# The last group's v read into k's buffer, the exponential put aside to a later slot, and other places for W4's last read and the sums of W3's blocks

## The chip, the cores and the metric

One core of one Trainium2 chip. The metric is the device time of the whole kernel in microseconds, here the median of three runs. Its engines are named as in the profile: PE (matmul; PEld is its load of weights), DVE (vector), ACT (scalar), POOL (GpSimd) and SP, which here only issues transfers. Each engine takes its own instructions in program order and waits on semaphores for the others.

## The reference

x is 2048 tokens by 576 channels, all in fp32. A layer norm of x feeds two branches, and their results are added to x:

```python
def _A_ref(x, wqkv, wo):                     # attention
    qkv = (x @ wqkv).reshape(B, S, 3, H, Dh) # H = 32 heads of Dh = 18
    idx = pos[:, None] - arange(8) * 2       # 8 keys per query, every second token back
    kg, vg = k[:, :, idx_c, :], v[:, :, idx_c, :]
    logits = einsum("bhsd,bhswd->bhsw", q, kg) * scale   # idx < 0 masked
    attn = softmax(logits)
    o = einsum("bhsw,bhswd->bhsd", attn, vg)
    return o.reshape(B, S, D) @ wo
def _B_ref(x, w1, w2, w3, w4):               # mixer MLP
    h = gelu(layernorm(x) @ w1)
    hs = shifts_of_quarters(h) @ w2          # four quarters of channels, shifted +1 -1 +2 -2 tokens
    x1 = x + hs
    return x1 + gelu(layernorm(x1) @ w3) @ w4   # w3: 576 x 4608, w4: 4608 x 576
xn = layernorm(x)
return x + _A_ref(xn, wqkv, wo) + _B_ref(xn, w1, w2, w3, w4)
```

## The kernel before

Every fp32 product on PE is made of products of two parts: each operand is split into a high part (rounded to the fp32r format, mostly by ACT) and a low part (what is left, mostly by DVE).

**Stages.** QKV: xn times wqkv; q, k and v go to a DRAM buffer qkvd. Then W1, the shifts and W2. Then W3, gelu and W4 for a part of the 4608 hidden channels in a plain loop of 32 units (L960). Then the round loop (L1130): 20 rounds q = 0 to 19, for the rest. Last the output projection by wo. Transfers are issued by SP, but for those that add to DRAM, which POOL issues (L837).

**Attention** runs on DVE beside all of this, from the plain loop on to round 14 at the latest. It is a generator, `attention` (L677), over 8 groups of heads. For a group g: logits by products and sums (L735, L738), the mask, the maximum and its subtraction (L745 to L749), the exponential on ACT (L753, over the tile L), then, a group late, `av(g - 1)` (L699): sum of L (L702), reciprocal (L703), scaling (L705), eight products with v (L711) and seven sums (L715), and the write of the result from tile po to DRAM od by SP (L717; its rows are pieces of 72 floats). q, k and v of a group are read by `load` from qkvd on SP (L692; k and v have a second, leading piece, L695). Each of q, k, v has one buffer, so a read waits until the group ahead is done with the tile: q and k of g + 1 are asked for when the logits of g are issued, v of g when av(g - 1) is.

**bg(us)** (L763) takes the next steps of that generator. It is called after every step of the loops with a budget of microseconds (1.6 in the rounds, less what DVE already got in that step, `spent`), and each step yields its estimated cost. A step that yields None sets `hold`: no later step is issued until a call with `late`, which in the rounds is the one after P6, but not in round 9.

**A round** takes a pair of 128-channel blocks of the hidden layer for one half of the tokens (rounds 0 to 9 the first, 10 to 19 the second, with the pairs in reverse order). P1 to P7 are its seven products of 7 matmuls each (L1065) by a Strassen-like scheme: operands A and S are blocks and combinations of W3 (tiles w3a, w3s), B and T blocks and combinations of the tokens (tiles x1n and xt). Results gather in PSUM banks cc and pass over ACT (`keep`, L1071) and DVE (`z_add`, L1075); gelu is on ACT (L795, L796, L801, L802), the low part on DVE (L807). D0 to D7 are the products of the round before with W4, 12 matmuls each (L832), one for each block of 128 tokens. Their two PSUM banks are emptied in turn, by DVE (L841) for some token blocks and by ACT and POOL (L836, L837) for others; D(n + 2) waits for the emptying of D(n).

The order of a round is written as a string; the ordinary one is `P1 P2 D0 P6 D1 P5 D2 P7 D3 P4 D4 P3 D5 D6 D7`, that of round 9 `P1 P2 P6 P5 P7 D0 P4 P3 D1 ... D7`, that of round 10 `D0 D1 P1 P2 D2 P6 ...`. `at("P7", f)` puts f behind that step on all engines. What is put so:

- `load_w4` (L559): W4 of this pair into two odd halves of the Y tile, on SP; `split_w4`: its high part by ACT (L566) and its low part by DVE (L569), which frees the landing place.
- `load_pair` (L910, L913): the raw block of W3 of a later round into w3st, six issues. `split_a` makes w3a of it (L926, L928 on ACT, L929 on POOL, L932 on DVE), `combine` (L921) four sums in place on DVE, and then `split_s` makes w3s.
- Round 9 reads the seven token operands of the second half (`get_op`, L881, L883: four issues each), and rounds 9 and 10 split them (`split_op`: L892 to L894 on ACT, L594 on DVE), B11 first.
- Rounds 15 to 18 prepare the output projection: `load_o` reads od (L1113), `o_turn` transposes it on DVE (L160, L161), `put_o` writes it to DRAM xd (L168), `read_xo` (L173) reads it back. Round 19 loads wo (L1101, L205).

A transfer on SP also waits until the one issued eight before it has landed, since their completions share eight semaphores.

Of the kernel before, what the change touches and what calls it, by code (L numbers as in the profile page):

```python
# [10 lines left out]
AF = mybir.ActivationFunctionType  # L11
# [46 lines left out]
def fused_block(ctx, tc, x, wqkv, wo, w1, w2, w3, w4, out):  # L58
# [618 lines left out]
    def attention(ap):  # L677
# [19 lines left out]
            return t  # L697

        def av(g):  # L699
            L, v = Ls[g], vs[g]  # L700
            Lf = L.rearrange("p j h w -> p (j h) w")
            dve.tensor_reduce(den[g], Lf, axis=AX.X, op=ALU.add)  # L702
            dve.reciprocal(den[g], den[g])  # L703
            yield 0.8
            dve.tensor_tensor(Lf, Lf, den[g][:, :, None].to_broadcast([128, TPP * GH, W]),  # L705
                              op=ALU.mult)
            yield 0.6
            for w in range(W):
                vv = v[:, DIL * w:DIL * w + TPP, :].rearrange("p j (h d) -> p (j h) d", d=HD)
                dst = prod if w else o  # L710
                dve.tensor_tensor(dst, vv, Lf[:, :, w:w + 1].to_broadcast([128, TPP * GH, HD]),  # L711
                                  op=ALU.mult)
                yield 1.35
                if w:
                    dve.tensor_tensor(o, o, dst, op=ALU.add)  # L715
                    yield 1.35
            sp.dma_start(od.rearrange("(p j) d -> p j d", p=128)[:, :, g * GC:(g + 1) * GC],  # L717
                         po[:, 0, :].rearrange("p (j c) -> p j c", c=GC))
# [5 lines left out]
        for g in range(NG + 1):  # L724
            if g < NG:
                q, k = qs[g], ks[g]
                L = Ls[g] = ap.tile([128, TPP, GH, W], F32, name="L", bufs=2)
                Lf = L.rearrange("p j h w -> p (j h) w")
                Lw = Lf.rearrange("p x w -> p w x")
                qf = q.rearrange("p j d -> p (j d)")  # L730
                for w, n in ((0, 1), (1, 1), (2, 2), (4, 2), (6, 2)):
                    dst = po[:, 2 - n:2, :]
                    win = bass.AP(tensor=k.tensor, offset=k.offset + DIL * w * GC,
                                  ap=[list(k.ap[0]), [DIL * GC, n], [1, TPP * GC]])
                    dve.tensor_tensor(dst, qf[:, None, :].to_broadcast([128, n, TPP * GC]), win,  # L735
                                      op=ALU.mult)
                    yield 0.15 + 1.2 * n
                    dve.tensor_reduce(Lw[:, w:w + n, :],  # L738
                                      dst.rearrange("p w (x d) -> p w x d", d=HD),
                                      axis=AX.X, op=ALU.add)  # L740
                    yield 0.15 + 1.2 * n
                if g + 1 < NG:
                    qs[g + 1], ks[g + 1] = load("q", 0, g + 1, False), load("k", 1, g + 1, True)
                mx = den[g] = ap.tile([128, TPP * GH], F32, name="mx", bufs=2)
                dve.tensor_tensor(L, L, mask4, op=ALU.add)  # L745
                yield 0.6
                dve.tensor_reduce(mx, Lf, axis=AX.X, op=ALU.max)
                yield 0.6
                dve.tensor_tensor(Lf, Lf, mx[:, :, None].to_broadcast([128, TPP * GH, W]),  # L749
                                  op=ALU.subtract)  # L750
                yield 0.6
                yield None
                act.activation(L, L, AF.Exp, scale=float(HD) ** -0.5)  # L753
                if g == 0:
                    yield 4.0
            if g:
                yield from av(g - 1)
                if g < NG:
                    vs[g] = load("v", 2, g, True)

    state = {"gen": None, "debt": 0.0, "hold": False, "done": False}

    def bg(us, late=True):  # L763
        if state["gen"] is None or state["done"]:
            return
        state["debt"] = min(state["debt"] + us, 4.0)
        while state["debt"] > 0 and (late or not state["hold"]):
            cost = next(state["gen"], False)
            if cost is False:
                state["done"] = True  # L770
                return
            state["hold"] = cost is None
            state["debt"] -= cost or 0.0


    def temp(t, n=512):
# [125 lines left out]
    def pair(q):  # L902
        return q if q < NWP else 2 * NWP - 1 - q
# [226 lines left out]
    for q in range(NQ):  # L1130
# [6 lines left out]
        if z == -1:  # L1137
# [3 lines left out]
            wop = tc.tile_pool(name="wop", bufs=1, reuse_waits="tile")  # L1141
            wopool = wop.__enter__()
            Wo = wopool.tile([128, 10, D], F32R, name="Wo")
            load_w4(p)
            for k in range(5):
                load_wo(k)
        if q == NWP:
# [17 lines left out]
        def at(it, f, *args):  # L1165
            plan.setdefault(it, []).append(lambda: f(*args))
# [45 lines left out]
        elif z < -1:  # L1212
            at("P1", load_w4, p)
            at("D1", split_a, n, (0, 1))
            at("D2", split_a, n, (2,))
            at("P7", combine, n)
            at("D3", split_w4, p, 0)
            at("P4", gelu22)
            at("P4", split_w4, p, 1)
# [5 lines left out]
            if z < -2:  # L1225
                at("D6", load_pair, q + 2 + (q == NWP - 2))
        else:
            at("D2", split_w4, p)
            at("D3", gelu22)
            at("D4", low22)  # L1230
            at("D5", gelu12)
            at("D6", low12)
# [9 lines left out]
        if -4 <= z < -1:  # L1242
            at("P1", put_o, z + 4)
        if z == -2:
            at("D7", put_o, 3)

        if z == -1:
# [134 lines left out]
```

## Time and profile before

| | us |
|---|---|
| median of three runs | 1306.22 (1305.91 to 1307.12) |
| the profiled execution, its time | 1301.97 |
| span of its trace | 1300.2 |
| mean granted clock of PE | 0.993 |
| PE busy in the span | 1266.0 |
| DVE busy | 944.6 |
| ACT busy | 598.2 |
| POOL busy | 245.2 |

The span is what the trace covers of one profiled execution; the execution's own time holds a little more at both ends. The three runs without a profile lie some 4 us above it. In rows of the timeline the first number is the start in the span, the second the length from the first instruction's start to the last one's end, then the engine, the line, operation, `out<-in`, shapes, and how many instructions the row groups; in brackets the idle time ahead of it and who ended it. A row of waits says who waited, for whom, then the sum in microseconds, the number of times and the longest. "SPq" is the issue of a transfer on SP. A row of transfers gives KB and the microseconds from issue to landing.

### The profile page before, as it was taken

How to read it: one execution, taken by the hardware profiler on the slowest of the kernel's cores; microseconds unless marked ns; L12 is line 12 of the kernel's file. 1: busy time of each engine (PE TensorE's matmuls, PEld its weight loads, DVE VectorE, ACT ScalarE, POOL GpSimd, SP SyncE). 2: the span in 40 equal slices, each digit the busy share in tenths (PEclk: the TensorE clock that was granted, in tenths of full speed). 3: DMA queues.
4: the chain of work that ended last, by engine and by line, in shares of the span. 5: the costliest groups of instructions: out<-in, count | busy, mean ns of one | idle time of the engine just before them, and what ended most of it. 6: DMA issues, size and time to landing. Idle time of an engine off the chain costs nothing.

```text
span 1300.2 us, 19681 instructions
## 1 busy us (share of the span) xinstructions
PE 1266.0 (97%) x7538; PEld 1161.7 (89%) x7538; DVE 944.6 (73%) x1261; ACT 598.2 (46%) x952; POOL 245.2 (19%) x358
## 2 busy tenths in 40 slices
PE   8999999999999999999999999999959999999999
PEld 8999998899888998989899889999848999988898
DVE  6456535778469999999999889999859654665442
ACT  3322226526534434344346656556546555554530
POOL 2011100021221212222221222222112222222100
PEclk9999999999999999999999999999979999999999
DMA  7646874256887878988788777776796658899972
GB/s 210 156 111 143 172 166 144 71 147 177 203 247 152 174 170 202 233 145 223 146 205 185 136 171 159 154 161 112 161 228 106 129 110 180 174 209 195 255 242 83
DMA packets 201374, 219.16 MB, mean 169 GB/s; under 512 B 79152, under 2 KB 137744, under 8 KB 201152
## 3 DMA queue, kind: packets, MB, share of 16 engines
q1 hardware_dynamic: 168912, 151.57, 41.0%
q0 software_dynamic: 32368, 66.34, 31.9%
q8 instruction: 59, 0.97, 0.3%
q14 instruction: 35, 0.29, 0.1%
HBM read 119.73 MB, written 107.28 MB: 175 GB/s over the span
## 4 chain that ended last, share of the span: by engine, by line
PE 78%; DMA 10%; DVE 4%; issue 4%; ACT 2%; SPq 1%; POOL 0%; DVEq 0%; POOLq 0%; ACTq 0%
PE ps L832 27%; PE ps L214 16%; PE cc L1065 13%; PE p L813 13%; PE ps L466 4%; PE ps L313 3%; DMA w3st<-in_B_w_dram 2%; DMA x1n<-xn 1%; DMA yd<-Y 1%; DMA xn<-st 1%; DMA xt<-xn 1%; DMA w3a<-w3st 1%; DMA xt<-xd 1%; DMA wr<-in_A_wo_dram 1%; PE ps L481 1%
## 5 line engine op out<-in xcount | busy, mean ns | idle before, releaser
L832 PEld LDWEIGHTS ps<-w,c 128*128 128x128 f32 x3456 | 474.5, 188 | 27.5 <-DVE Y L841 8.8
L832 PE MATMUL ps<-w,c 128*128 128x288 f32 x3456 | 486.1, 295 | 10.8 <-DVE Y L841 7.0
L837 POOL DMA_DIRECT2D yd<-Y x154 | 137.0, 894 | 464.7 <-ACT Y L836 388.4
L836 ACT COPY Y<-ps 128x576 f32<-128x576 f32 x154 | 97.9, 636 | 151.4 <-PE ps L832 96.5
L807 DVE TENSOR_TENSOR c<-Y,c 128x512 fp32r<-128x512 f32 x144 | 98.4, 685 | 58.8 <-ACT Y L796 42.3
L214 PE MATMUL ps<-WQ,xt 128*128 128x432 f32 x672 | 134.8, 360 | 0.0
L214 PEld LDWEIGHTS ps<-WQ,xt 128*128 128x128 f32 x672 | 125.6, 188 | 5.7
L1065 PE MATMUL cc<-xt,w3s 128*128 128x512 f32 x420 | 108.3, 398 | 13.5 <-DVE Y L1075 13.5
L841 DVE TENSOR_TENSOR Y<-ps,Y 128x576 f32<-128x576 f32 x108 | 81.2, 751 | 49.2 <-PE ps L832 49.0
L1065 PEld LDWEIGHTS cc<-xt,w3s 128*128 128x128 f32 x420 | 76.7, 190 | 27.6 <-DVE Y L1075 14.0
L711 DVE TENSOR_TENSOR po<-v,L 128x1152 f32<-128x1152 f32 x64 | 86.1, 1353 | 14.7 <-DMA v<-qkvd 13.8
L735 DVE TENSOR_TENSOR po<-q,k 128x2304 f32<-128x2304 f32 (+1 forms) x40 | 82.9, 2073 | 13.9 <-issue 11.6
L795 ACT ACTIVATE c<-p 128x512 fp32r<-128x512 f32 x64 | 38.2, 597 | 115.8 <-PE p L813 115.8
L738 DVE TENSOR_REDUCE L<-po 128x128 f32<-128x2304 f32 (+1 forms) x40 | 82.8, 2069 | 0.4
L1071 ACT COPY Y<-cc 128x512 f32<-128x512 f32 x60 | 35.1, 584 | 97.4 <-PE cc L1065 94.1
L121 POOL TENSOR_TENSOR rs<-rs,mhalf 128x1 f32<-128x1 f32 x48 | 30.9, 643 | 258.8 <-DVE rs L120 148.0
L715 DVE TENSOR_TENSOR po<-po 128x1152 f32<-128x1152 f32 x56 | 75.8, 1353 | 0.8
L323 ACT COPY stg<-ps 128x864 f32<-128x864 f32 x24 | 21.2, 881 | 102.8 <-PE ps L214 60.5
L1065 PE MATMUL cc<-x1n,w3a 128*128 128x512 f32 (+1 forms) x280 | 67.9, 393 | 0.0
L1065 PEld LDWEIGHTS cc<-x1n,w3a 128*128 128x128 f32 (+1 forms) x280 | 51.6, 188 | 10.3
L214 PE MATMUL ps<-W,h 128*128 128x288 f32 x384 | 53.5, 295 | 0.0
L813 PE MATMUL p<-xt,w3s 128*128 128x512 f32 x224 | 52.4, 390 | 0.0
(188 smaller groups left out, 1892.6 us busy)
## 6 DMA issues: line engine op xcount, KB each, us to landing
yd<-Y POOLq DMA_DIRECT2D x156, 288.0 KB, 5.2
Y<-in_B_w_dram SPq DMA_DIRECT2D x27, 576.0 KB, 6.7
w3st<-in_B_w_dram SPq DMA_DIRECT2D x52, 256.0 KB, 6.3
qkvd<-stg SPq DMA_DIRECT2D x24, 432.0 KB, 3.5
yd<-ev POOLq DMA_DIRECT2D x26, 288.0 KB, 6.4
xd<-st SPq DMA_DIRECT2D x16, 320.0 KB, 6.0
xd<-big SPq DMA_DIRECT2D x16, 320.0 KB, 7.4
w3st<-in_B_w_dram SPq DMA_DIRECT2D x76, 64.0 KB, 6.5
```

The lines of the kernel that those rows point to most:

```text
L214: pe.matmul(ps[:, h, :n], xs(a), ws(b, h), start=i == 0, stop=i == len(PAIRS) - 1)
L711: dve.tensor_tensor(dst, vv, Lf[:, :, w:w + 1].to_broadcast([128, TPP * GH, HD]), op=ALU.mult)
L715: dve.tensor_tensor(o, o, dst, op=ALU.add)
L735: dve.tensor_tensor(dst, qf[:, None, :].to_broadcast([128, n, TPP * GC]), win, op=ALU.mult)
L738: dve.tensor_reduce(Lw[:, w:w + n, :], dst.rearrange("p w (x d) -> p w x d", d=HD), axis=AX.X, op=ALU.add)
L807: dve.tensor_tensor(h[:, 1, :], g, h[:, 0, :].bitcast(F32), op=ALU.subtract)
L813: pe.matmul(ps, W3[f][:, w, :], x1n[b][:, a, :], start=n == 0, stop=n == len(PAIRS) - 1)
L832: pe.matmul(ps[:, k, :HF], h[:, col], w[:, p, k * HF:(k + 1) * HF], start=n == 0, stop=n == len(seq) - 1)
L836: act.copy(e.rearrange("p (h c) -> p h c", h=2), ps[:, :, :HF])
L837: pool.dma_start(yd[t], e, accum_op=ALU.add)
L841: dve.tensor_tensor(yv, ps[:, :, :HF], yv, op=ALU.add)
L1065: pe.matmul(ps, WX[w][:k, v, SLOT[w], :], area[sb][xk][:k, a, :], start=onto is None and i == 0, stop=last and i == len(HALVES) - 1, skip_ ...
```

## The change

Four things are done.

1. v of the last group (g = 7) is no longer read into v's buffer behind av(6), but into k's buffer, asked for as soon as the last logits are issued. The other groups are read as before.
2. The exponential is no longer issued where the generator reaches it, and the generator no longer stops there: it is put aside in `state["exp"]` and issued by the next `late` call of bg, or at the next group's exponential, or ahead of av(7).
3. W4 of the last round is read at D7 of round 18, ahead of that round's `put_o`, and no longer at the start of round 19; in round 19 its split and the first gelu come a step later.
4. `combine` goes from P7 to D3 in rounds 1 to 8 and 11 to 18, ahead of the first half of `split_w4`.

```diff
@@ -697,6 +697,8 @@
             return t
 
         def av(g):
+            if g == NG - 1:
+                exp_now()
             L, v = Ls[g], vs[g]
             Lf = L.rearrange("p j h w -> p (j h) w")
             dve.tensor_reduce(den[g], Lf, axis=AX.X, op=ALU.add)
@@ -749,28 +751,36 @@
                 dve.tensor_tensor(Lf, Lf, mx[:, :, None].to_broadcast([128, TPP * GH, W]),
                                   op=ALU.subtract)
                 yield 0.6
-                yield None
-                act.activation(L, L, AF.Exp, scale=float(HD) ** -0.5)
+                exp_now()
+                state["exp"] = lambda L=L: act.activation(L, L, AF.Exp, scale=float(HD) ** -0.5)
+                if g == NG - 1:
+                    vs[g] = load("k", 2, g, True)
                 if g == 0:
                     yield 4.0
             if g:
                 yield from av(g - 1)
-                if g < NG:
+                if g < NG - 1:
                     vs[g] = load("v", 2, g, True)
 
-    state = {"gen": None, "debt": 0.0, "hold": False, "done": False}
+    state = {"gen": None, "debt": 0.0, "exp": None, "done": False}
+
+    def exp_now():
+        if state["exp"]:
+            state["exp"]()
+            state["exp"] = None
 
     def bg(us, late=True):
         if state["gen"] is None or state["done"]:
             return
+        if late:
+            exp_now()
         state["debt"] = min(state["debt"] + us, 4.0)
-        while state["debt"] > 0 and (late or not state["hold"]):
+        while state["debt"] > 0:
             cost = next(state["gen"], False)
             if cost is False:
                 state["done"] = True
                 return
-            state["hold"] = cost is None
-            state["debt"] -= cost or 0.0
+            state["debt"] -= cost
 
 
     def temp(t, n=512):
@@ -1141,7 +1151,6 @@
             wop = tc.tile_pool(name="wop", bufs=1, reuse_waits="tile")
             wopool = wop.__enter__()
             Wo = wopool.tile([128, 10, D], F32R, name="Wo")
-            load_w4(p)
             for k in range(5):
                 load_wo(k)
         if q == NWP:
@@ -1213,7 +1222,7 @@
             at("P1", load_w4, p)
             at("D1", split_a, n, (0, 1))
             at("D2", split_a, n, (2,))
-            at("P7", combine, n)
+            at("D3", combine, n)
             at("D3", split_w4, p, 0)
             at("P4", gelu22)
             at("P4", split_w4, p, 1)
@@ -1225,8 +1234,8 @@
             if z < -2:
                 at("D6", load_pair, q + 2 + (q == NWP - 2))
         else:
-            at("D2", split_w4, p)
-            at("D3", gelu22)
+            at("D3", split_w4, p)
+            at("P4", gelu22)
             at("D4", low22)
             at("D5", gelu12)
             at("D6", low12)
@@ -1242,6 +1251,7 @@
         if -4 <= z < -1:
             at("P1", put_o, z + 4)
         if z == -2:
+            at("D7", load_w4, NPL + pair(q + 1))
             at("D7", put_o, 3)
 
         if z == -1:
```

The orders of PE and POOL stay the same. In the rows below names have the kernel's own counters, and the lines of the changed kernel are 2 to 10 higher: L719 is L717 of before, L891 L881, L920 L910, L931 L921.

SP, rounds 8 and 9, before: from the W3 block's last issues and W4 of round 9 through the first two operands to the third.

```order
L559 DMA Y<-in_B_w_dram 128x2x576
L881 DMA x1n_6401<-xn_98 128x2x512
L883 DMA x1n_6401<-xn_98 32x512 x3
L881 DMA x1n_6401<-xn_98 128x2x512
L883 DMA x1n_6401<-xn_98 32x512 x3
L717 DMA od<-po 2048x1x72
L692 DMA v<-qkvd 128x1152
L695 DMA v<-qkvd 128x1008
L881 DMA xt<-td1T_105 128x2x512
```

The same place now, beginning with W4 of round 7.

```order
L559 DMA Y<-in_B_w_dram 128x2x576
L692 DMA k<-qkvd 128x1152
L695 DMA k<-qkvd 128x1008
L920 DMA w3st<-in_B_w_dram 128x2x256 x2
L923 DMA w3st<-in_B_w_dram 32x2x256 x4
L559 DMA Y<-in_B_w_dram 128x2x576
L920 DMA w3st<-in_B_w_dram 128x2x256 x2
L923 DMA w3st<-in_B_w_dram 32x2x256 x4
L719 DMA od<-po 2048x1x72
L559 DMA Y<-in_B_w_dram 128x2x576
L891 DMA x1n_6402<-xn_98 128x2x512
L893 DMA x1n_6402<-xn_98 32x512 x3
```

The last read of v, two pieces, stood between the second and the third operand of round 9. It stands behind W4 of round 7 now, into k; and od's write of group 6 has come from behind the second operand to a place ahead of W4 of round 9.

DVE, round 18, from the low part of a gelu to the evacuation of a D step, before:

```order
L807 TENSOR_TENSOR c_10357<-Y,c_10357 128x512
L921 TENSOR_TENSOR w3st<-w3st 128x3x128 x4
L160 STREAM_TRANSPOSE big_9924<-Y 128x16x32
L161 STREAM_TRANSPOSE big_9924<-Y 128x4x32
L569 TENSOR_TENSOR w_10285<-Y,w_10285 128x2x576
L841 TENSOR_TENSOR Y<-ps_10423,Y 128x576
```

and now:

```order
L817 TENSOR_TENSOR c_10357<-Y,c_10357 128x512
L160 STREAM_TRANSPOSE big_9924<-Y 128x16x32
L161 STREAM_TRANSPOSE big_9924<-Y 128x4x32
L931 TENSOR_TENSOR w3st<-w3st 128x3x128 x4
L569 TENSOR_TENSOR w_10285<-Y,w_10285 128x2x576
L851 TENSOR_TENSOR Y<-ps_10423,Y 128x576
```

The two transposes stood behind the four sums of W3's block and stand ahead of them now; the low part of W4 still follows.

SP, end of round 18 and beginning of round 19, before:

```order
L559 DMA Y<-in_B_w_dram 128x2x576
L168 DMA xd<-big_9923 32x20x128 x4
L1113 DMA Y<-od 32x576 x4
L168 DMA xd<-big_9924 32x20x128 x4
L559 DMA Y<-in_B_w_dram 128x2x576
L1101 DMA wr<-in_A_wo_dram 128x576 x4
```

and now:

```order
L559 DMA Y<-in_B_w_dram 128x2x576
L168 DMA xd<-big_9923 32x20x128 x4
L1123 DMA Y<-od 32x576 x4
L559 DMA Y<-in_B_w_dram 128x2x576
L168 DMA xd<-big_9924 32x20x128 x4
L1111 DMA wr<-in_A_wo_dram 128x576 x4
```

W4's read and the four writes of `put_o` have changed places.

## The prediction

> **What bounds the kernel now.** I read the page's totals and its chain of waits first, then the waits by engine, then the timeline of each engine around the longest wait, and last the windows and the transfers there.
>
> ```profile
> PE 1266.0 (97%) x7538; PEld 1161.7 (89%) x7538; DVE 944.6 (73%) x1261; ACT 598.2 (46%) x952; POOL 245.2 (19%) x358
> PE 78%; DMA 10%; DVE 4%; issue 4%; ACT 2%; SPq 1%; POOL 0%; DVEq 0%; POOLq 0%; ACTq 0%
> ```
>
> PE works 97% of the span, and this change leaves the matmuls alone: it can win only PE's gaps, which are 1300.2 − 1266.0 = 34.2 us, or make new ones. The waits tell whose they are: of PE first, and then the one row of DVE's that matters.
>
> ```profile
> PE cc L1065 <- DVE Y L1075: 13.5, 1, 13.5
> PE ps L832 <- DVE Y L841: 7.0, 7, 1.5
> PE cc L1065 <- ACT Y L1071: 2.7, 1, 2.7
> ...
> DVE po L711 <- DMA v<-qkvd: 13.8, 1, 13.8
> ```
>
> One gap of 13.5 us is over a third of it all. Seven short ones wait for DVE's evacuation L841. One of 2.7 us waits for ACT. The long one lies in round 9, where the halves of the tokens change. PE there:
>
> ```profile
> 938.93 1.77 PE L1065 MATMUL cc<-x1n,w3s 128*128 128x512 f32 x7
> 940.54 1.75 PE L832 MATMUL ps<-w,c 128*128 128x288 f32 x12
> 942.13 1.79 PE L1065 MATMUL cc<-xt,w3a 128*128 128x512 f32 x7
> 957.45 3.29 PE L1065 MATMUL cc<-xt,w3s 128*128 128x512 f32 x7 [13.54 <-DVE Y L1075]
> 960.57 9.95 PE L832 MATMUL ps<-w,c 128*128 128x288 f32 x72
> 970.88 3.57 PE L832 MATMUL ps<-w,c 128*128 128x288 f32 x24 [0.36 <-ACT Y L836]
> 975.39 1.86 PE L832 MATMUL ps<-w,c 128*128 128x288 f32 x12 [0.94 <-ACT Y L836]
> ```
>
> DVE in the same stretch, then SP, which issues the transfers:
>
> ```profile
> 939.67 0.69 DVE L705 TENSOR_TENSOR L<-L,mx 128x512 f32<-128x512 f32 x1
> 954.17 2.63 DVE L711 TENSOR_TENSOR po<-v,L 128x1152 f32<-128x1152 f32 x2 [13.80 <-DMA v<-qkvd]
> 956.71 0.68 DVE L1075 TENSOR_TENSOR Y<-cc,Y 128x512 f32<-128x512 f32 x1
> ```
>
> ```profile
> 935.77 0.45 SPq L559 DMA_DIRECT2D Y<-in_B_w_dram  x1
> ...
> 945.87 0.53 SPq L717 DMA_DIRECT2D od<-po  x1
> 946.45 2.22 SPq L692 DMA_DIRECT2D v<-qkvd  x1
> ```
>
> The causal chain is plain. v of the last group has one buffer, free only when av of group 6 has ended, as it had before L705 of group 7 at 939.67. Its read stands on SP behind W4 and eight issues of operand reads, goes out at 946.45 and lands at 954.17. DVE has stood in L711 since 940.3, with L1075 behind it, the sum that frees a bank of cc for the next product: PE waits for that until 957.45. ACT:
>
> ```profile
> 945.83 1.06 ACT L892 ACTIVATE x1n<-x1n 128x1024 fp32r<-128x1024 f32 x1 [4.51 <-DMA x1n<-xn]
> ...
> 947.59 0.63 ACT L894 ACTIVATE x1n<-x1n 64x512 fp32r<-64x512 f32 x1
> 962.37 0.64 ACT L836 COPY Y<-ps 128x576 f32<-128x576 f32 x1 [14.15 <-PE ps L832]
> ...
> 967.96 1.04 ACT L892 ACTIVATE xt<-xt 128x1024 fp32r<-128x1024 f32 x1
> ```
>
> The windows (busy time of PE, PEld, DVE, ACT, POOL, then granted clock, share of the DMA engines, GB/s), and the two transfers of one size that landed in 930 to 975:
>
> ```profile
> 943.00:957.00 14.00, 0.92 (x4) 0.38 (x3) 2.83 (x3) 2.31 (x3) 0.00 (x0) 0.64 1.04 285
> ...
> 965.00:970.00 5.00, 5.00 (x38) 4.80 (x37) 4.94 (x6) 4.92 (x8) 0.87 (x1) 1.00 0.75 112
> ```
>
> ```profile
> Y<-in_B_w_dram SPq DMA_DIRECT2D x1, 576.0 KB, 7.2
> ...
> od<-po SPq DMA_DIRECT2D x1, 576.0 KB, 5.5
> ```
>
> While PE stands still the DMA engines are full: whatever ends the wait for v will meet the operand reads. And from 962.37 on ACT is the one that is full (4.92 of 5.00): PE's next two gaps, 0.36 and 0.94, wait for it.
>
> **A: v into k's buffer, and the exponential that stops nothing.** k of group 7 is last read by the logits, so the read of v goes out in round 7, two rounds ahead of its use, far longer than the 7.7 us that it took here (946.45 to 954.17); L711 finds it there. The 13.54 us do not all go, since another chain stands close behind: operand B11 lands at 945.83, ACT's three activations on it end at 947.59 + 0.63 = 948.22, 2.4 us later, and only then, in ACT's order, comes the evacuation L836 that frees a psum bank. Before, L836 began at 962.37 and from it ACT ran without a break to the evacuation that released PE at 975.39: 975.39 − 962.37 = 13.0 us. If that stretch keeps its length and follows B11's three activations at once, the new time of its end is B11's landing + 2.4 + 13.0.
>
> When B11 lands: in the new order od's write stands ahead of W4 and B11 on SP. At least its issue, 0.5 us, is added: 946.3, the end at 961.7, a gain of 13.7. At most it holds the operand up by its whole 5.5 us as well: 951.8, the end at 967.2, a gain of 8.2. Between: the two v reads, 576 + 504 KB, leave this stretch, but they were issued behind B11, so they do not help it; od's 0.59 MB at 285 GB/s take 2.1 us. With 0.5 + 2.1 B11 lands at 948.4, the end is 963.8. I take **−11.5** (13.7 … 8.2). The later operands are close: T2's read goes out when the eighth issue before it has landed, as od's did before (945.87, behind B11's 945.83), so near 948.4, lands some 7 us later (W4's row), near 955.5, and ACT wants it at 967.96 − 11.6 = 956.4.
>
> [...]
>
> **B: W4 of the last round is issued a slot earlier.** SP now, and the ACT and PE rows that follow from it:
>
> ```profile
> 1202.21 1.94 SPq L559 DMA_DIRECT2D Y<-in_B_w_dram  x1
> ...
> 1210.73 1.15 ACT L566 CAST w<-Y 128x1152 fp32r<-128x1152 f32 x1 [5.58 <-DMA Y<-in_B_w_dram]
> ...
> 1207.95 1.75 PE L832 MATMUL ps<-w,c 128*128 128x288 f32 x12
> 1212.42 2.79 PE L1065 MATMUL cc<-xt,w3a 128*128 128x512 f32 x7 [2.72 <-ACT Y L1071]
> ...
> 1217.28 1.78 PE L1065 MATMUL cc<-xt,w3s 128*128 128x512 f32 x7
> ```
>
> ACT stands 5.58 us in the cast with the copy of cc behind it, and PE waits for the copy. The cast now stands behind that copy and an evacuation, and the transfer goes out ahead of put_o's four issues, about 11 us earlier. PE took 1217.28 − 1207.95 = 9.33 for 12 + 7 + 12 matmuls whose pitch is 1.59, 1.61 and 1.59 in the rows of round 9 (942.13 − 940.54, 940.54 − 938.93): 4.8. The gain is at most this difference, 4.5; at least the wait alone, 2.7, if the slower matmuls have another cause. put_o itself goes out 1.94 us later, for the tiles that the output stage reads last. I take **−4.5** (2.7 … 4.5).
>
> The clock is in that term. The seven matmuls behind the wait of 2.72 us took 2.79 instead of 1.79, and behind that of 13.54 they took 3.29. [...]
>
> **C: the sums of W3's blocks move from P7 to D3.** DVE in round 16 and the three alike gaps of PE in rounds 16 to 18:
>
> ```profile
> 1135.61 2.34 DVE L921 TENSOR_TENSOR w3st<-w3st 128x384 f32<-128x384 f32 x4 [2.40 <-issue]
> 1137.87 0.70 DVE L160 STREAM_TRANSPOSE big<-Y 128x512 f32<-128x512 f32 x1
> 1138.50 0.27 DVE L161 STREAM_TRANSPOSE big<-Y 128x128 f32<-128x128 f32 x1
> ...
> 1140.73 3.44 PE L832 MATMUL ps<-w,c 128*128 128x288 f32 x24 [1.45 <-DVE Y L841]
> 1166.02 3.44 PE L832 MATMUL ps<-w,c 128*128 128x288 f32 x24 [0.95 <-DVE Y L841]
> 1191.81 3.44 PE L832 MATMUL ps<-w,c 128*128 128x288 f32 x24 [1.47 <-DVE Y L841]
> ```
>
> L921 waits 2.40 us, and the two transposes that follow it wait with it; L841, for which PE stands, comes behind all of them. In the new order the transposes run inside that wait. What they add behind L921 is 0.7 + 0.3, by starts 1138.69 − 1137.87 = 0.82; each gap loses that: 3 × 0.82 = **−2.4**. Bounds: 0, if L921's wait moves by as much, since "issue" names no releaser; −3.9, all three gaps. In the other rounds an attention product goes into the place of the transposes, hidden in the same way.
>
> **D: small changes.** In rounds 3 and 5 attention's reads now stand ahead of W4 on SP; B's row is the pattern of a late W4: a wait of 5.58 on ACT became 2.72 on PE, so 2.86 are absorbed. W4 delayed by three issues (946.45: 2.2, others 0.5) is about 3 us late at most: +0.4 (0 … 1.5). Attention's work on DVE, no longer stopped at the exponential, comes a few products earlier in the first part, where DVE is nearly full and PE has no gap to lose:
>
> ```profile
> 450.00:650.00 200.00, 199.57 (x1185) 181.28 (x1184) 192.81 (x175) 77.48 (x123) 45.33 (x52) 1.00 0.86 184
> ```
>
> The amount of work is the same, paid out by the same budget per slot, so I take 0 to 2, +0.5. One of the seven L841 gaps, in round 1, stands behind a W4 that now meets other transfers: −0.5 (0 … −1.2).
>
> Sum: −11.5 − 4.5 − 2.4 + 0.4 + 0.5 − 0.5 = **−18.0**, from the profiled 1301.97 to 1284.0. That execution is 4.25 below the median of the runs, 1306.22; the same distance is kept: **1288.2**. Best ends of all terms: −13.7 − 4.5 − 3.9 − 1.2 = −23.3, 1282.9; worst: −8.2 − 2.7 + 1.5 + 2.0 = −7.4, 1298.8.
>
> **Rivals.** *DMA bounds the switch* (0.25): the engines were at 1.04 with 285 GB/s from 943 to 957, so if what PE waited for is bytes, only v's 1.11 MB leave, 3.9 us, and the operands set the rest: 1306.2 − 3.9 − 4.5 − 2.4 + 0.4 = 1295.8. For it: the full window. Against: B11 had landed at 945.83 and PE waited for DVE, not for an operand; most reads of that window are wanted only in the stretch behind 962.
>
> *SP stands on od, slower* (0.05): od's write now stands in SP's order ahead of W4 and all operand reads of round 9. It can go out only when group 6's last L715 has ended; if attention is behind there, everything behind od waits.
>
> ```profile
> SPq L717 <- DVE po L715: 74.8, 5, 33.8
> ```
>
> SP has stood up to 33.8 us there. With that at the switch, −18.0 + 33.8: 1322. It decides once that wait is over 18 us: SP reached W4, od's new place, at 935.77, so from an L715 that ends later than about 954. Against it: before, group 6 was done ahead of 939.67, and attention only runs earlier now.
>
> *Nothing changes* (0.04): an operand read takes v's place at the switch and all of A goes back there, the last W4 meets put_o's transfers and lands as late as before, and L921's wait moves with it, so that A, B and C are 0 and D is left: 1306.6. Against it: three separate covers would have to fail at once.
>
> **Chances.** Forecast with its own range 1283 to 1294: 0.66; DMA 0.25; SP 0.05; no change 0.04. What a measurement of this kernel can tell from no change is 0.2%, 2.6 us. Faster takes the first two, 0.91; same 0.04; slower 0.05. The range reaches from a little below the best sum, since gaps of under a microsecond may close too, to above the DMA case: 1280.5 to 1299.5.
>
> **What would show it.** Right: no row of L711 waits for v; PE's gap before P3 of round 9 is under 3 us; ACT is busy from L892 on B11 without a break to D1 of round 10, which ends near 964; L566 of the last round waits for nothing and PE's 2.72 is gone; L160 stands ahead of L921 and the three gaps are near 0.6, 0.1 and 0.6. Wrong: a wait of ACT on an operand longer than 3 us (DMA), SP waiting on L715 in round 9, PE's gaps on L841 in the first part grown by more than 2 us in sum, or cc waiting for another DVE operation in round 9.

## The result, and the profile after

| | before | changed |
|---|---|---|
| median of six runs on the same chips, us | 1305.39 (1303.65 to 1307.12) | 1294.29 (1290.82 to 1296.31) |
| profiled execution, its time, us | 1301.97 | 1294.18 |
| span of its trace, us | 1300.2 | 1292.4 |
| PE busy, us | 1266.0 | 1267.1 |
| mean granted clock of PE | 0.993 | 0.994 |

The ratio is 0.9914, interval 0.9898 to 0.993: the change makes the kernel faster by 11.1 us in the medians, where 18.0 were predicted. The two traces stand 7.8 us apart; why that is less comes with the experiments.

The waits of PE in the changed kernel, and one of DVE, by the same view as before:

```profile
PE cc L1075 <- ACT Y L1081: 6.3, 1, 6.3
PE ps L842 <- DVE Y L851: 5.6, 8, 1.2
PE ps L842 <- ACT w L566: 2.0, 1, 2.0
...
DVE po L713 <- DMA od<-po: 7.6, 1, 7.6
```

The wait of 13.5 has become one of 6.3, the 2.7 of the tail has gone, and there is a new one, 2.0, for ACT's cast of W4. DVE no longer waits for v. It waits for **od**, the write of group 6's result. PE, then DVE, ACT and SP at the switch of token halves in round 9:

```profile
944.66 1.75 PE L842 MATMUL ps<-w,c 128*128 128x288 f32 x12
952.73 3.35 PE L1075 MATMUL cc<-xt,w3a 128*128 128x512 f32 x7 [6.32 <-ACT Y L1081]
955.88 2.43 PE L1075 MATMUL cc<-xt,w3s 128*128 128x512 f32 x7
...
972.97 1.85 PE L842 MATMUL ps<-w,c 128*128 128x288 f32 x12 [0.94 <-ACT Y L846]
```

```profile
940.63 0.68 DVE L707 TENSOR_TENSOR L<-L,mx 128x512 f32<-128x512 f32 x1
948.92 1.36 DVE L713 TENSOR_TENSOR po<-k,L 128x1152 f32<-128x1152 f32 x1 [7.60 <-DMA od<-po]
950.20 0.68 DVE L1085 TENSOR_TENSOR Y<-cc,Y 128x512 f32<-128x512 f32 x1
```

```profile
950.91 0.63 ACT L811 ACTIVATE c<-Y 128x512 fp32r<-128x512 f32 x1 [8.68 <-DVE Y L1085]
951.57 0.63 ACT L812 ACTIVATE Y<-Y 128x512 f32<-128x512 f32 x1
952.11 0.57 ACT L1081 COPY Y<-cc 128x512 f32<-128x512 f32 x1
...
959.95 0.64 ACT L846 COPY Y<-ps 128x576 f32<-128x576 f32 x1 [5.00 <-PE ps L842]
```

```profile
939.81 0.52 SPq L719 DMA_DIRECT2D od<-po  x1
940.38 5.09 SPq L559 DMA_DIRECT2D Y<-in_B_w_dram  x1
945.58 0.41 SPq L891 DMA_DIRECT2D x1n<-xn  x1
```

L713's first product of a group writes the half of the tile po from which od's write of the group before still reads. od goes out at 939.81 and L713 starts at 948.92, 9.1 us later. Behind L713 on DVE stands L1085, behind that on ACT the gelu L811, L812 and the copy L1081 that PE needs. k's buffer did its part: L713 now reads k, and no wait names v. W4's issue, directly behind od's, took 5.09 us, where it took 0.45 before (935.77 in the prediction's rows); B11's read waited for that on SP.

The second place is round 0. The small accumulating transfer, and the window from 728 to 734 (columns as before), of the kernel before:

```profile
w3a<-w3st POOLq DMA_DIRECT2D x1, 48.0 KB, 2.3
```

```profile
728.00:734.00 6.00, 6.00 (x38) 5.49 (x37) 5.54 (x8) 5.03 (x9) 1.70 (x2) 1.00 0.20 27
```

and of the changed kernel, with the transfers that are new there, DVE and PE:

```profile
od<-po SPq DMA_DIRECT2D x1, 576.0 KB, 8.5
v<-qkvd SPq DMA_DIRECT2D x1, 576.0 KB, 9.5
...
v<-qkvd SPq DMA_DIRECT2D x1, 504.0 KB, 6.1
...
w3a<-w3st POOLq DMA_DIRECT2D x1, 48.0 KB, 4.6
```

```profile
728.00:734.00 6.00, 6.00 (x37) 5.46 (x37) 5.91 (x8) 4.67 (x8) 1.70 (x2) 1.00 1.21 295
742.00:749.00 7.00, 6.14 (x21) 5.25 (x20) 6.66 (x7) 1.18 (x4) 0.05 (x1) 0.52 0.93 203
```

```profile
735.96 2.34 DVE L931 TENSOR_TENSOR w3st<-w3st 128x384 f32<-128x384 f32 x4 [1.89 <-DMA w3a<-w3st]
```

```profile
741.68 0.53 PE L842 MATMUL ps<-w,c 128*128 128x288 f32 x2 [2.00 <-ACT w L566]
743.07 2.77 PE L842 MATMUL ps<-w,c 128*128 128x288 f32 x10 [0.86 <-DVE w L569]
```

Attention, no longer stopped at the exponential, has come to the end of group 4 a round earlier, and its write of od and read of v fall into a stretch where the DMA engines had been at 0.20. They are at 1.21 now, 48 KB take twice as long, and L931 cannot begin; ACT's w3s and cast of W4 follow late, PE stands for 2.0 and 0.86 us, and the clock granted behind it is 0.52.

Rounds 16 to 18 and the tail look as the prediction drew them. DVE in round 16, then PE and ACT in round 19:

```profile
1130.69 0.70 DVE L160 STREAM_TRANSPOSE big<-Y 128x512 f32<-128x512 f32 x1
1131.32 0.27 DVE L161 STREAM_TRANSPOSE big<-Y 128x128 f32<-128x128 f32 x1
1133.57 2.34 DVE L931 TENSOR_TENSOR w3st<-w3st 128x384 f32<-128x384 f32 x4 [1.98 <-issue]
```

```profile
1204.28 1.75 PE L842 MATMUL ps<-w,c 128*128 128x288 f32 x12
1205.87 1.79 PE L1075 MATMUL cc<-xt,w3a 128*128 128x512 f32 x7
```

```profile
1206.61 1.16 ACT L566 CAST w<-Y 128x1152 fp32r<-128x1152 f32 x1
```

The transposes run ahead of the sums, inside L931's wait. In the tail the cast waits for nothing and PE goes on without a gap.

### The profile page after: what moved, and what is told of

It reads as the page before. It is cut to its first block, busy times and chain, and to the rows that moved or that the text cites. A ratio compares the mean times of both kernels' runs of the same rounds, so it can differ in the third digit from the quotient of the medians.

```text
span 1292.4 us, 19686 instructions
## 1 busy us (share of the span) xinstructions
PE 1267.1 (98%) x7538; PEld 1163.1 (90%) x7538; DVE 944.7 (73%) x1261; ACT 598.7 (46%) x952; POOL 246.3 (19%) x358
## 4 chain that ended last, share of the span: by engine, by line
PE 74%; DMA 8%; issue 7%; DVE 6%; ACT 2%; SPq 2%; POOL 1%; DVEq 0%; POOLq 0%; ACTq 0%
PE ps L842 26%; PE ps L214 16%; PE cc L1075 12%; PE p L823 12%; PE ps L466 4%; PE ps L313 3%; DMA yd<-Y 2%; DMA w3st<-in_B_w_dram 1%; DMA Y<-in_B_w_dram 1%; DMA w3a<-w3st 1%; DVE w L569 1%; DMA od<-po 1%; PE ps L481 1%; DVE w3st L931 1%; DMA w3s<-w3st 1%
## 5 line engine op out<-in xcount | busy, mean ns | idle before, releaser
L842 PE MATMUL ps<-w,c 128*128 128x288 f32 x3456 | 486.4, 295 | 11.9 <-DVE Y L851 5.6
L846 ACT COPY Y<-ps 128x576 f32<-128x576 f32 x154 | 98.1, 637 | 141.8 <-PE ps L842 90.4
L851 DVE TENSOR_TENSOR Y<-ps,Y 128x576 f32<-128x576 f32 x108 | 81.1, 751 | 48.8 <-PE ps L842 48.5
L737 DVE TENSOR_TENSOR po<-q,k 128x2304 f32<-128x2304 f32 (+1 forms) x40 | 82.9, 2073 | 16.1 <-issue 10.9
L1081 ACT COPY Y<-cc 128x512 f32<-128x512 f32 x60 | 35.1, 585 | 100.7 <-PE cc L1075 94.9
L717 DVE TENSOR_TENSOR po<-po 128x1152 f32<-128x1152 f32 x56 | 75.8, 1353 | 0.9
L713 DVE TENSOR_TENSOR po<-v,L 128x1152 f32<-128x1152 f32 x56 | 75.6, 1352 | 0.7
L323 ACT COPY stg<-ps 128x864 f32<-128x864 f32 x24 | 21.2, 882 | 102.8 <-PE ps L214 55.8
L1075 PEld LDWEIGHTS cc<-x1n,w3a 128*128 128x128 f32 (+1 forms) x280 | 51.6, 188 | 10.3
```

The lines of the kernel that those rows point to most:

```text
L842: pe.matmul(ps[:, k, :HF], h[:, col], w[:, p, k * HF:(k + 1) * HF], start=n == 0, stop=n == len(seq) - 1)
L846: act.copy(e.rearrange("p (h c) -> p h c", h=2), ps[:, :, :HF])
L851: dve.tensor_tensor(yv, ps[:, :, :HF], yv, op=ALU.add)
L1075: pe.matmul(ps, WX[w][:k, v, SLOT[w], :], area[sb][xk][:k, a, :], start=onto is None and i == 0, stop=last and i == len(HALVES) - 1, skip_ ...
```

## The experiments

PE's 7538 matmuls are the same, in the same order, in all kernels here. So a stage can be measured in each trace as the time from the start of one matmul to the start of another, which takes the gaps and the slower clock behind them together. The table, worked out from the traces, has numbers 4200 to 4300 for round 0 (around the gap at 741), 4300 to 4400 (around 760), 4400 to 5300 (rounds 2 to 8), 5300 to 5650 (the switch), 6500 to 6850 (rounds 16 to 18), 6900 to 6960 (the tail), and the whole. Parts have the numbers of the section on the change; "q tile" is explained below.

| kernel | round 0 | near 760 | rounds 2 to 8 | switch | 16 to 18 | tail | all |
|---|---|---|---|---|---|---|---|
| before | 18.8 | 18.1 | 149.6 | 75.8 | 61.9 | 14.7 | 1295.4 |
| before, second profile | 18.8 | 17.8 | 149.6 | 78.4 | 67.4 | 12.1 | 1303.6 |
| before + 4 | 18.8 | 18.2 | 149.8 | 76.3 | 60.2 | 16.4 | 1296.8 |
| before + 1 | 18.8 | 16.7 | 149.3 | 72.8 | 61.5 | 14.9 | 1292.7 |
| before + 1, 3, 4 | 18.9 | 18.5 | 150.2 | 73.7 | 63.8 | 10.1 | 1291.6 |
| changed | 23.5 | 16.7 | 150.8 | 69.3 | 60.7 | 10.1 | 1287.5 |
| changed, second profile | 22.2 | 16.7 | 150.6 | 70.6 | 60.2 | 10.1 | 1292.8 |
| changed without 4 | 21.6 | 16.7 | 150.9 | 69.0 | 65.7 | 10.1 | 1290.8 |
| changed, od of group 4 later | 18.8 | 20.8 | 150.8 | 69.9 | 59.6 | 10.1 | 1290.7 |
| changed + q tile | 21.4 | 16.7 | 150.8 | 65.3 | 59.4 | 10.1 | 1280.8 |
| changed + q tile, B11 first | 19.9 | 16.7 | 150.4 | 63.3 | 60.1 | 10.1 | 1280.8 |
| before + 1, 3, 4 + q tile | 18.8 | 18.5 | 149.8 | 64.9 | 60.1 | 10.1 | 1278.1 |
| the same, B11 first | 18.8 | 21.2 | 149.8 | 62.5 | 59.6 | 10.1 | 1286.8 |

Not in a column is the first part, up to matmul 4200. It took 727.9 to 736.8 us, the kernel before 728.7 and 730.7, the changed one 728.4 and 733.5: two executions of one kernel differ there by several microseconds. Totals of single traces are therefore read with care, and stages apart from it.

**v into k's buffer alone.**

```diff
                 act.activation(L, L, AF.Exp, scale=float(HD) ** -0.5)
+                if g == NG - 1:
+                    vs[g] = load("k", 2, g, True)
...
-                if g < NG:
+                if g < NG - 1:
                     vs[g] = load("v", 2, g, True)
```

> The kernel before with part 1 of the change alone: v of group 7 goes into k's buffer; the exponential, W4's last read and the sums of W3's blocks stay. Theory 'od' (the first product of the last group writes the tile po that od's write of group 6 still reads, so L711 waits for the landing of od): od goes out at about 945.9 behind eight operand issues as before and lands 5.5 us later, near 951.4, where v had landed at 954.17; the gap of 13.54 us shrinks by 2.7 us to about 10.8, its releaser is od, and the time is 2.7 us lower; round 0 and the tail are as before. Rival 'v' (the prediction: v was all that DVE waited for): the gap goes down to about 2 us and the time by 8 to 13 us.

Measured: ratio 0.9994, interval 0.9978 to 1.001; the switch is 3.0 us shorter than in the first profile of before. The interval of the ratio holds both the 2.7 us expected and no gain at all, so it is the trace that decides. DVE and PE of this kernel:

```profile
951.40 2.63 DVE L711 TENSOR_TENSOR po<-k,L 128x1152 f32<-128x1152 f32 x2 [10.71 <-DMA od<-po]
```

```profile
954.68 3.35 PE L1067 MATMUL cc<-xt,w3s 128*128 128x512 f32 x7 [10.45 <-DVE Y L1077]
```

od went out behind eight operand issues as before and ended the wait at 951.40, the moment expected; PE's gap is 10.45. The prediction's own expectation, 8 to 13 us, falls: v was the last of two waits, and the other ended 2.8 us ahead of it.

**The stop at the exponential put back** (parts 1, 3 and 4 on the kernel before).

```diff
-                exp_now()
-                state["exp"] = lambda L=L: act.activation(L, L, AF.Exp, scale=float(HD) ** -0.5)
+                yield None
+                act.activation(L, L, AF.Exp, scale=float(HD) ** -0.5)
```

> The changed kernel with part 2 undone: attention stops at the exponential again as before; v of group 7 in k's buffer, W4's last read and the sums of W3's blocks as changed. Theory 'traffic' (without the stop, od's write and the reads of v came to round 0, where they filled the DMA engines and held up the small transfer w3a<-w3st, L921, ACT and PE, at 740 us): round 0 loses nothing, the first product waits for od at the switch as in the run above (-2.7), the three gaps of rounds 16 to 18 and the tail win what they won in the changed kernel (-1.2 and -4.3): about 8 us under before, near the changed kernel's own time, by another sum. Rival 'chance' (the loss in round 0 is how one execution happens to go): the stall of 2.0 us at 740 comes here as well, and the time is 3 to 4 us above the changed kernel's.

Measured: 1296.62, ratio 0.9941 (0.9921 to 0.9961), 7.2 us under its runs of before. Round 0 is 18.9: no loss there, and the stall of "chance" did not come. The switch is 73.7, as with part 1 alone; what part 2 wins there by putting od nine issues earlier, ahead of W4 and eight issues of operand reads (73.7 to 69.3 and 70.6), it gives back in round 0.

**The result of group 7 gathered in q's tile**, free after the last logits, so that nothing writes what od's write reads.

```diff
+            out = po[:, 0, :]
+            if g == NG - 1:
+                out = qs[g].rearrange("p j d -> p (j d)")
+            o = out.rearrange("p (x d) -> p x d", d=HD)
```

> The changed kernel, but av of group 7 gathers its result in q's tile, which is free after the last logits, and not in po, which od's write of group 6 still reads. Theory 'od': L713 waits for nothing; the next thing is B11, which lands some 6 us after its issue at 945.6, near 952, so that the evacuation L846 begins near 954.4 and not at 959.95: 5.6 us less than the changed kernel, and no gap of PE over 3 us in round 9 that waits for DVE. Rival 'DMA' (the engines are full and set the switch by their bytes): PE's gap only moves to the next product, ACT waits 5 us or more for an operand, and the time is within 1.5 us of the changed kernel's.

Measured: 1289.34, ratio 0.989 (0.987 to 0.991). The switch is 65.3, 4.0 and 5.3 under the two profiles of the changed kernel, a little less than the 5.6 expected (the intervals of the two ratios, 0.989 and 0.9914, overlap), and no DVE row waits for od there. ACT in this kernel shows what is next:

```profile
951.17 1.06 ACT L906 ACTIVATE x1n<-x1n 128x1024 fp32r<-128x1024 f32 x1 [7.11 <-DMA x1n<-xn]
...
953.70 0.61 ACT L850 COPY Y<-ps 128x576 f32<-128x576 f32 x1
```

It waits for B11 and then does its three activations and the evacuation, the chain on which the prediction had built A. "DMA" was right in one point, the wait of over 5 us for an operand, and wrong in the time.

**Part 4 undone**: `combine` at P7 again, all else as changed.

```diff
-            at("D3", combine, n)
+            at("P7", combine, n)
             at("D3", split_w4, p, 0)
```

> The changed kernel with part 4 undone: the sums of W3's blocks stand at P7 again. Theory 'transposes': the three gaps of rounds 16 to 18 go back from 1.05, 0.84 and 0.76 to about 1.45, 0.95 and 1.47 us, +1.2; in round 9 the reads of W3's block, od and W4 go out up to 4 us earlier, since w3st comes free earlier, which takes up to 2 us from the wait for od: between -1 and +1.2 us against the changed kernel. Rival (the sums' place matters in all middle rounds): +2.4 us or more, with new gaps of PE in rounds 1 to 8 or 11 to 14.

Measured: 1297.44, ratio 0.9943 (0.9917 to 0.997). Rounds 16 to 18 take 65.7 instead of 60.7 and 60.2, more than expected, with gaps of 2.60, 1.50 and 2.00 us; the switch is unchanged. The expected earlier od brought nothing there, and no new gap came to the other rounds.

**Part 4 alone** on the kernel before, the same line the other way round.

> The kernel before with part 4 alone, the sums of W3's blocks at D3. Theory 'transposes': the gaps of 1.45, 0.95 and 1.47 us in rounds 16 to 18 lose up to 0.82 each, 1.2 to 2.4 us less than before in its trace, nothing else moves. Rival: the sums come later, so w3s, and the next reads into w3st, come later; new gaps of PE on ACT or DVE in the middle rounds, or a later v in round 9: not under before, or above it by 1 us or more.

Measured: 1303.06, ratio 0.998 (0.9961 to 0.9999). Rounds 16 to 18 take 60.2 instead of 61.9 and 67.4, and the rival's later reads do not show: switch 76.3, between the two profiles of before. The tail's gap grew to 3.49 us in this trace, W4 still being late there.

**od of group 4 kept back** in the changed kernel from round 0 to round 1, behind W4.

```diff
+            while g == 4 and not state["go"]:
+                yield None
             sp.dma_start(od.rearrange("(p j) d -> p j d", p=128)[:, :, g * GC:(g + 1) * GC],
...
+            if cost is None:
+                return
             state["debt"] -= cost
...
+        state["go"] = q > 0
         for it in ORDERS.get(q, ORDER).split():
```

> The changed kernel, but the write of od of group 4 and the read of v of group 5 that follows it are kept back from round 0 to round 1, behind W4, where they stood before. Theory 'traffic': w3a<-w3st lands in about 2.3 us and not 4.6, L931 does not wait for it, PE's 2.00 us at 741 and the slow matmuls behind it are gone (4.5 us), and a gap of about 1.2 us near 760 comes back: 3 us less than the changed kernel. Rival 'stop': the loss comes from attention's work on DVE in another order, and stays: no difference to the changed kernel.

Measured: 1298.2, ratio 0.9933 (0.9912 to 0.9953), not under the changed kernel. The place was right: w3a<-w3st takes 2.3 us again, round 0 is 18.8. (The run keeps attention's next work on DVE back in round 0 too. That the transfers did it, and not that work, is read from the changed kernel's trace, where L931 waits for the landing of the 48 KB.) But the gain went to the next place; DVE and PE of this kernel in round 1:

```profile
756.67 2.56 DVE L739 TENSOR_TENSOR po<-q,k 128x2304 f32<-128x2304 f32 x1 [4.74 <-DMA od<-po]
```

```profile
759.95 3.25 PE L846 MATMUL ps<-w,c 128*128 128x288 f32 x12 [2.34 <-DVE Y L855]
```

The logits' products of two offsets at once write both halves of po and wait for od there too. So the expectation of 3 us fell, by the mechanism that the switch had shown. 18.8 + 20.8 is 39.6, the changed kernel had 40.2 and 38.9.

**B11 first, od last**, with q's tile, in the changed kernel.

```diff
+            at("P1", get_op, 1, "B11")
             at("P1", load_w4, p)
...
+            at("P3", lambda: state["od"]())
```

> The changed kernel with the result of group 7 in q's tile, and in round 9 the read of B11 issued first, W4 behind it, and od's write of group 6 behind all seven operands. Theory 'B11': ACT waited 7.1 us for B11 with q's tile alone, because od and W4 stood ahead of it on SP; now B11 goes out 5 us earlier and that wait goes: 4 to 5 us less than 1289.34. Rival 'DMA': the engines carry the same bytes, the next operands and W4 are late instead, PE stands at a D step for ACT or for W4: within 1.5 us of 1289.34.

Measured: 1287.17, ratio 0.9852 (0.9826 to 0.9878). The switch is 63.3, 2.0 less than with q's tile alone, and ACT's wait for B11 is 2.84 us instead of 7.11. Under half of the expected 4 to 5: ACT now waits 1.03 us for the second operand, a sign that bytes set a part of it; how much was not separated.

**The stop put back, and q's tile** (the two repairs together).

> v of group 7 in k's buffer, the result of group 7 in q's tile, W4's last read and the sums of W3's blocks as changed, and the stop at the exponential as before: the changed kernel with part 2 undone and without the wait for od. Theory 'od': round 0 loses nothing; B11 is issued ahead of od and lands near 946.0, its three activations end at 948.4, the evacuation L836 follows at once instead of at 962.37, and ACT's 13.0 us follow that: 14 us at the switch, 4.3 in the tail, 0 to 1.2 in rounds 16 to 18: 18 to 19 us under before, some 3 to 4 under the run with the stop removed and q's tile (1289.34). This is the sum that the prediction gave to the change. Rival 'DMA': the later operands come too late, ACT waits for them inside its 13 us, and the switch wins no more than in that run (8 to 9): 1289 or more.

Measured: 1288.11, ratio 0.9854 (0.983 to 0.9878), 17.6 us under its runs of before, 1305.74, where 18 to 19 were expected. Switch 64.9, tail 10.1, rounds 16 to 18 60.1, round 0 18.8. The run with the stop removed and q's tile was 14.5 under its own runs of before, 1303.87. So the medians show 3.1 of the 3 to 4 us expected between the two, but the intervals of the ratios, 0.9854 and 0.989, overlap. The switch brought less than the 14 expected: it is 10.9 us under the first profile of before and only 0.4 under the run with the stop removed, as "DMA" had it, and ACT waits 1.13 and 0.61 us for later operands inside its stretch.

**The same with B11 first and od last.**

> The run with the stop at the exponential and q's tile (1288.11), and in addition B11's read first in round 9, W4 behind it and od's write behind all operands. Theory 'B11': ACT waited 5.5 us for B11 there and 1.1 for T2, and a gap of 2.2 us with slow matmuls followed; without od's bytes ahead of T2 the gap goes and the switch wins 2 to 3 us more: 1285 to 1286. Rival 'ACT' (the 13 us of ACT's work at the switch set it from here on): nothing, within 1 us of 1288.1.

Measured: 1285.93, ratio 0.9831 (0.9801 to 0.986), the lowest of all, and the shortest switch, 62.5. The expected step of 2 to 3 us is there in the switch (64.9 to 62.5) and in the medians (2.2), though the two intervals of the ratio overlap. In its trace PE stands 2.65 us near 760 (21.2 in the table), where the other kernels with the stop stood 1.50 at most; why is open.

**A second profile of each kernel.**

> The kernel before, a second profile. The first one's time, 1301.97, lay 3.4 under the median of its runs, and the changed kernel's profile on its median, so that the two traces differ by 7.8 us and the medians by 11.1. Theory 'luck': the stretch up to 560 us, where several other runs were 1 to 3 us later than the first profile, is later by 1 to 3 us here too, with the same gaps at 741, 760, in round 9, in rounds 16 to 18 and in the tail. Rival: the 3.4 us lie at the switch or in round 0, so that the change won more there than the two traces show.

> The changed kernel, a second profile. Theory 'traffic': L931 waits for w3a<-w3st in round 0 again and PE has a gap of 1 to 2 us near 741 with slow matmuls behind it; L713 waits 7 to 9 us for od in round 9. Rival 'chance': one of the two is not there.

Measured: 1310.25 and 1299.4, one run each. The first half of "luck" holds, with 2 us more in the first part; but most of the 8.3 us between the two profiles of before lie elsewhere, 2.5 at the switch and 5.4 in rounds 16 to 18, while the tail is 2.6 shorter. PE there in the second profile of before:

```profile
1146.03 4.97 PE L832 MATMUL ps<-w,c 128*128 128x288 f32 x24 [2.02 <-DVE Y L841]
1174.11 4.93 PE L832 MATMUL ps<-w,c 128*128 128x288 f32 x24 [2.22 <-DVE Y L841]
1201.98 3.44 PE L832 MATMUL ps<-w,c 128*128 128x288 f32 x24 [2.06 <-DVE Y L841]
```

The gaps of part 4's place are not 1.45, 0.95 and 1.47 in every execution; when they reach 2 us, 24 matmuls can take 4.97 instead of 3.44. The first profile of before lies 3.4 us under the median of its runs, the second 4.3 above that of its own. So neither is the rule, and one trace of each kernel could not give the 11.1 us. In the changed kernel both losses came again: 22.2 in round 0, and a wait of 8.4 us for od.

## Why the prediction was right or wrong

The time, 1294.29, lies in the range, and the direction was right; the likeliest value, 1288.2, was 6 us too low. That the range held it is in part luck: it was drawn wide enough to take in the case "DMA". The forecast's own range ended at 1294, and 1294.29 is nearer to that rival's 1295.8. Of the signs named, three came: L711 (L713 now) does not wait for v, L566 of the last round waits for nothing, and L160 stands ahead of the sums. Two did not: PE still stands 6.32 us in round 9, one product earlier than before, and ACT has a break of 5.00 us ahead of L846. Per part, with the means of the profiles in which the part is off or on:

| term | predicted | measured, from the table |
|---|---|---|
| A, the switch | −11.5 (−8.2 to −13.7) | −6.9 (76.8 to 69.9) |
| B, the tail | −4.5 | −4.4 (14.5 to 10.1) |
| C, rounds 16 to 18 | −2.4 (0 to −3.9) | −3.7 (64.1 to 60.4) |
| D, round 0, near 760, rounds 2 to 8 | +0.4 | +3.8 (+4.1, −1.3, +1.1) |
| sum | −18.0 | −11.2 |

(A, D: three profiles with neither part 1 nor 2, and two of the changed kernel; B: four with the old place of W4's last read; C: four with the old place of the sums, and two of the changed kernel.) The sum agrees with the medians' 11.1, more closely than the scatter allows: the switch of one kernel differs by 2.5 us between two profiles, rounds 16 to 18 by 5.4.

**A, the step that failed**: "the read of v goes out in round 7 ...; L711 finds it there", and from this, that the next chain is B11's. Between the two stood a third, od. Its issue, 945.87, and its 5.5 us were both in the quoted rows: 951.4, only 2.8 us ahead of v. What was not asked is who else must be done before L711 may write po. The wait names only what came last, and the tile that an instruction writes has its own readers. The range's lower end, 8.2, counted od as a load on the queue in front of B11, not as a wait of DVE, so the measured 6.9 lies outside it. The steps behind it can be seen where q's tile takes od's wait away. PE's first product of round 9 in the kernel before, and in the changed kernel with q's tile, where the last row is the release that was at 975.39 before:

```profile
932.47 3.40 PE L1065 MATMUL cc<-x1n,w3a 128*128 128x512 f32 x14
```

```profile
935.20 3.40 PE L1079 MATMUL cc<-x1n,w3a 128*128 128x512 f32 x14
...
967.59 1.85 PE L846 MATMUL ps<-w,c 128*128 128x288 f32 x12 [0.35 <-ACT Y L850]
```

Counted from these starts, ACT begins with B11 (945.83 and 951.17) 2.6 us later, as much as the prediction had put, and PE is released 10.5 us earlier, near its 11.5. The switch took 65.3 and 64.9 with q's tile, 11.5 and 11.9 under the mean of before. ACT's stretch from L836 to PE's release was 972.97 − 959.95 = 13.0 in the changed kernel too. But the 2.6 us did not come from the prediction's two terms, 0.5 for od's issue and 2.1 for its bytes. With q's tile W4's issue behind od took 4.51 us instead of 0.45, so that B11's read went out 4.8 us later after the start of the round, and then it landed in 7.4 us instead of 9.6. That the two nearly made up the forecast sum is luck.

**B** was right in mechanism, and in size on the mean. The slower matmuls behind the gap went with it: 4.4 and not the wait's 2.7. They count as busy time of PE, so the prediction's bound, the 34.2 us in which PE is not busy, had left them out. In single traces the gap was 1.68 to 3.49 us, with slow matmuls behind 2.72, 2.97 and 3.49 and none behind 1.68, and the term was worth 2.0 to 6.3.

**C** was right in mechanism, the transposes inside L921's wait. The size was not. In the first profiles the gaps became 1.05, 0.84 and 0.76, not about 0.6, 0.1 and 0.6, and the stage lost 1.2 us, half of the 2.4. On the mean it lost more, 3.7, since in other executions the gaps of the old place reach 2 us, and the cost of the slower matmuls behind them (24 in 4.97 us instead of 3.44, at a granted clock of 0.59) was left out.

**D, the other step that failed**: "the amount of work is the same, paid out by the same budget per slot". That holds for DVE's work. But the generator issues transfers too, and these 1656 KB came a round earlier into a stretch where the DMA engines had been at 0.20; a transfer of 48 KB on the path of W3's block became 2.3 us longer. With od and v kept back that loss is gone. The loss near 760, gone in the changed kernel, was foreseen in kind (−0.5 for −1.3), though the kernel with part 1 alone has 16.7 there too; the gap near 860 in rounds 2 to 8 (1.15 us, for DVE's L851) was only allowed for. The runs with the stop put back have 150.2, 149.8 and 149.8 there, so it comes with part 2. The traces point to od again. In the changed kernel:

```profile
850.71 2.56 DVE L737 TENSOR_TENSOR po<-q,k 128x2304 f32<-128x2304 f32 x1 [2.75 <-DMA od<-po]
```

```profile
860.86 3.44 PE L842 MATMUL ps<-w,c 128*128 128x288 f32 x24 [1.15 <-DVE Y L851]
```

The logits' product over two offsets waits for od there, by 2.4 to 2.9 us in all six traces with part 2 and in none without it, and DVE's work up to L851 follows with a break of only 0.53 us. That this wait makes the gap was not tried by a run.

**The rivals.** "DMA bounds the switch" gave 1295.8 and came near by number, but not by its mechanism: PE waited behind DVE for one write, and taking that wait away won 4.0 to 5.3 us of stage with the same bytes on the engines. Its other half, late operands, is true of the kernels with q's tile. "SP stands on od" did not come, as od was ready when SP reached it. At the switch od itself, always in the same pieces, landed in 4.9 to 5.6 us where it goes out behind the first operands, in 8.7 to 9.3 where it stands ahead of W4 and them, and in 9.7 and 10.3 behind all operands; what sets this was not separated, and no run here tried od in longer pieces.

## What to carry to other kernels

When a wait is to be taken away, list everything that the waiting instruction needs, the readers of the tile that it writes too, with the time at which each was done: the second to last is what remains. When work is moved earlier in a background stream, move its transfers in thought as well, and look at what small transfer on the critical path lies in the window that they will fill. Before a gap of one trace is used as a size, look at it in a second execution.

## What the runs showed of the hardware

PE's matmuls were slow behind gaps of 2 to 3 us. The 2.72 us of the tail was followed by seven in 2.79 us instead of 1.79, with a granted clock of 0.69 from 1212 to 1215; 2.02 and 2.22 us in the second profile of before were followed by 24 in 4.97 and 4.93 us instead of 3.44. The window of 1146 to 1150 there shows a granted clock of 0.59:

```profile
1146.00:1150.00 4.00, 3.97 (x19) 3.98 (x20) 4.00 (x7) 1.90 (x3) 1.19 (x3) 0.59 0.92 151
```

The gap of 2.06 in the same trace was followed by matmuls at full speed (24 in 3.44 us, a granted clock of 1.00 from 1200 to 1206), and so were one of 2.00 with part 4 undone and all single gaps of 1.73 and less in the rows read. So 2.02 is the shortest single gap with slow matmuls behind it here, and not every gap of that length had them. Two gaps close together did it with less: with q's tile, 1.11 and 0.86 us some 1.4 us apart in round 0 were followed by 10 matmuls in 2.77 us, while behind 1.15 and 0.86 in the same place, in the kernel with B11 first, 10 took 1.59. In the two rows of 24 a slow stretch cost 1.53 and 1.49 us, 0.76 and 0.67 of the gap ahead of it.

An issue on SP that followed od's write at once was a long one: 2.2 to 4.3 us behind the first seven of od's eight writes in the kernel before, 2.4 to 5.4 in the changed one, 1.3 to 5.9 over the thirteen traces, where the median issue on SP takes 0.47. Behind the last write, where the next issue came over 10 us later, it took 0.39 in both. The rows of the switch show it with v behind od (2.22 us before) and with W4 behind od (5.09 in the changed kernel). What SP waits for there is not shown.
